# Batch 3's x loads, casts and transposing DMA moved ahead in a hand-ordered attention and maxout kernel on Trainium2

## The chip, the cores and the metric

The kernel runs on one core of a Trainium2 chip. The core has a matrix engine (TensorE, PE in the profile, with its weight loads as PEld), a vector engine (VectorE, DVE), a scalar engine (ScalarE, ACT), a general engine (GpSimd, POOL) and a sync engine (SyncE, SP), which here issues nearly all DMAs. Every engine works through its own list of instructions in program order and waits on semaphores for what other engines and DMAs deliver. The metric is device time in microseconds (us) of one execution; less is better.

## What is computed

```python
# x (8, 8, 512, 64), state (8, 8, 32, 64), float32
scores = scale * x @ state.T            # per batch and head
a      = softmax(scores)
xread  = a @ state                      # 512 rows
a2     = softmax(scale * state @ x.T)
sread  = a2 @ x                         # 32 rows
attn   = concat([xread, sread], axis=2) # then heads side by side: (8*544, 512)
h1, h2 = attn @ w1, attn @ w2
out    = maximum(h1, h2) @ w_out        # (4352, 512) float32
```

## The kernel before, in words

One pass handles one of the 8 batches. For batch n the kernel loads x (two DMAs of 512 KB, four heads each, `load_x`, line 164), casts it to bf16 twice, forms the scores, their exponentials, the weights a and their transpose, and multiplies the state with the maxout weights once for all (`sw`), so that the two matrix layers of the batch work from 64 rows of state and the transposed a.

The two casts have two users. `cast_e(b, k)` (name `ce` in the table, line 103 in the profile, tile `xe`) casts two heads into the tile that the product for sread reads; there are four of them for a batch. `cast_b(b, g)` (name `cb`, line 103 too, tile `xb`) casts four heads into the tile that is transposed; there are two. `xt_dma(b)` (name `xtd`, line 239) is a DMA that reads all of `xb` and writes the transposed x into `xt`. The score product `sc_mm` (line 261) reads `xt`. So a batch's scores need both loads, both `cb` and `xtd`; its four `ce` are needed only later, by `sr_mm` (line 301).

Tile `xt` has two buffers, `xe` three, `xb` two. The big float buffers are shared: x of batch 3 lies in a buffer of its own until output 3 takes it, x of batch 4 takes over one that held half of w2, and x of batch 7 takes the one that held output 0. `store(b)` (line 470) is the 1 MB DMA of a batch's output.

Nothing reorders the program: the order in which the code calls the helpers is each engine's order. For the weights and batches 0 and 1, with the parts of batches 2 to 5 that run beside them, this order is the table ORDER (lines 23 to 45), read from left to right by the loop at line 647. A token is a name with its batch and part, a letter behind ">" chooses the engine (A is ACT, V is DVE, P is POOL), and a number behind "@" the PSUM bank. After the table, the loop at line 736 writes passes b = 2 to 6: first layer of batch b (`l1_mm`, line 377: 16 matmuls), then the scores of batch n = b + 1 (line 261), then products of the second layer (lines 428 and 434), the state product (line 354), sread (line 301). So the first thing that needs batch 3's transposed x is the score product in pass b = 2, right behind the 16 matmuls of line 377. `cb` of batch 4 and its `xtd` are written ahead of that pass (lines 734 to 739), behind the x loads of batch 5 (`ldx.5`), the last tokens of the table.

The names of buffers in the order listings: big_118 holds x of batch 3, big_110 x of batch 4, big_113 x of batch 5, big_109 output 0; xe_84, xb_90 and xt_88 are the tiles of batch 3, a_93 and at_101 those of batch 2; big_115 holds the differences of two halves of `sw` (`difference`, line 404).

Of the kernel before, what the change touches and what calls it, by code (L numbers as in the profile page):

```python
# [35 lines left out]
sw.1.0@0,5 swe.0.0.0>A swe.0.0.1>V sw.0.w@1,3 sw.1.w@7,6 cb.2.1>P swe.1.0.0>A swe.1.0.1>V xtd.2 wt.1>P p2.1@2 l1.0.6@4  # L36
swe.0.w.0>A re.0.6>V l1.0.3@0 l1.0.2@5 swe.0.w.1>A re.0.3>V swe.1.w.0>V mS.1>A l1.0.1@4 l1.0.0@1 p2.0@3 swe.1.w.1>V
mS.0>A Sd dif.0>P re.0.2>V re.0.1>A re.0.0>A p2o.0 l1.1.0@7 l1.1.1@6 l1.1.2@0 l1.1.3@5 re.1.0>V re.1.1>A re.1.2>A
rs.0.0>V rs.0.1>V re.1.3>A p2o.1 ldx.4.1 ldx.3.0 ldx.4.0 ldx.3.1 p1.0@1 k0.0>A p1.1@4 rs.0.2>V wt.2>V v00.0 p6.0
rs.0.3>V k0.1>A k1.0>A p5.0@7 wt.3>V v00.1 rs.1.0>V k2.0>A sc.2.0@6 exp.2.0>A sc.2.1@0 exp.2.1>A sw.2.0@5,3 red.2.0>V  # L40
mul.2.0>P red.2.1>V swe.2.0.0>A swe.2.0.1>A ce.2.0>A ce.2.1>A ce.2.2>A ce.2.3>A p7.0 o7.0 v11.0 rs.1.1>V mul.2.1>P
p3.0 o3.0 rs.1.2>V atd.2 sw.2.w@6,2 swe.2.w.0>A v01.0 swe.2.w.1>A p4.0 o4.0 rs.1.3>V ce.3.0>P ce.3.1>P cb.3.0>P
ce.3.2>P ce.3.3>P cb.3.1>P v10.0>A store.0 xtd.3 dif.1>P sr.2@0 p6.1 k1.1>A sw.2.1@5,3 sre.2>V swe.2.1.0>A swe.2.1.1>V
p5.1@7 k2.1>A p7.1 o7.1 v11.1 p3.1 o3.1 v01.1 srt.2@0 srte.2>A p4.1 o4.1 v10.1>A ldx.5.0 ldx.5.1
"""

# [860 lines left out]
```

## Time and profile before

| what | us |
|---|---|
| median of 3 runs | 144.87 |
| the runs | 144.87, 231.15, 144.86 |
| profiled execution, its own time | 144.49 |
| its span in the trace | 142.7 |

The span is what the trace covers, from the first to the last instruction; the profiled execution's own time is 1.79 us more. The page lists, for each engine, how long it was busy, and for each stretch that one asks for the busy time in it. A wait is named by the engine that waited and by what released it. The chain is followed back from the last instruction: at each step, what released it. Matmuls are pipelined and their ends are modelled, so the starts of two matmuls tell more of PE's pace than the end of one.

### The profile page before, as it was taken

To read this page: it belongs to the slowest core of one execution; us is meant where nothing else is said; L and a number is where in the kernel's file an instruction comes from. 1 tells how busy PE (TensorE), PEld (TensorE's weight loads), DVE (VectorE), ACT (ScalarE), POOL (GpSimd) and SP (SyncE) were. 2 spreads that over 40 slices of the span, in tenths; PEclk is the share of its full clock that TensorE was granted. 3 is DMA by queue.
4 is the path that set the end of the run, shared out by engine and by line. 5 is a ranking of instruction groups with operands and counts; after the bars stand their busy time and mean duration, and the time that the engine had idled before them with its cause. 6 is when DMAs were issued, how large, how long until landed. Compare 5 with 4: busy or idle time off the path is not lost.

```text
span 142.7 us, 3661 instructions
## 1 busy us (share of the span) xinstructions
PE 134.8 (94%) x1442; PEld 95.1 (67%) x1442; DVE 104.5 (73%) x193; ACT 88.2 (62%) x172; POOL 72.4 (51%) x99
## 2 busy tenths in 40 slices
PE   6897999999999998999999999999999999999980
PEld 2475735456887764786678577857876786788860
DVE  3489979778999947974898489569948986847420
ACT  4357969887599445674874769086737745753220
POOL 4147335099019992699079909963980544200000
PEclk9999999999999999999999999999999999999999
DMA  4999999945999889979936999659217041502073
GB/s 128 337 365 395 387 384 386 341 80 102 179 330 276 299 172 293 135 189 275 403 129 122 211 356 199 146 207 238 43 38 294 2 78 71 225 0 78 12 246 119
DMA packets 36453, 29.50 MB, mean 207 GB/s; under 512 B 22609, under 2 KB 32337, under 8 KB 35537
## 3 DMA queue, kind: packets, MB, share of 16 engines
q1 hardware_dynamic: 36160, 29.10, 72.1%
q8 instruction: 12, 0.20, 0.5%
q10 hardware_dynamic: 272, 0.13, 0.3%
q14 instruction: 9, 0.07, 0.1%
HBM read 15.20 MB, written 8.91 MB: 169 GB/s over the span
## 4 chain that ended last, share of the span: by engine, by line
PE 75%; DMA 8%; DVE 5%; POOL 5%; ACT 2%; issue 2%; SPq 0%; POOLq 0%; DVEq 0%
PE bank L428 28%; PE bank L377 16%; PE bank L434 8%; PE bank L608 5%; DMA xt<-xb 4%; DVE big L404 4%; PE bank L354 4%; DMA big<-in_x_dram 3%; PE bank L261 3%; PE bank L475 2%; PE bank L517 2%; POOL xe L103 2%; PE bank L323 1%; POOL xb L103 1%; PE bank L550 1%
## 5 line engine op out<-in xcount | busy, mean ns | idle before, releaser
L277 POOL TENSOR_TENSOR a<-e,er 128x512 bf16<-128x512 bf16 x14 | 17.2, 1235 | 28.3 <-ACT big L99 20.9
L372 DVE TENSOR_SCALAR r<-bank 128x512 bf16<-128x512 f32 x32 | 21.9, 690 | 13.0 <-PE bank L377 12.6
L99 ACT COPY big<-bank 128x512 f32<-128x512 f32 (+2 forms) x40 | 21.8, 551 | 13.2 <-PE bank L434 5.5
L377 PE MATMUL bank<-at,sw 128*128 128x512 bf16 x128 | 29.5, 379 | 0.2 <-DVE sw L101 0.2
L428 PEld LDWEIGHTS <-big 128*128 128x128 bf16 x256 | 23.8, 97 | 6.1 <-DVE big L404 1.7
L99 ACT CAST sw<-bank 128x512 bf16<-128x512 f32 x36 | 20.1, 609 | 6.0 <-PE bank L354 6.0
L428 PE MATMUL bank<-big,big 128*128 128x256 bf16 x192 | 23.1, 273 | 0.1
L404 DVE TENSOR_TENSOR big<-bank,big 128x512 f32<-128x512 f32 (+1 forms) x25 | 16.5, 663 | 8.2 <-PE bank L434 7.8
L377 PEld LDWEIGHTS <-sw 128*128 128x128 bf16 x128 | 12.2, 97 | 13.5 <-ACT sw L99 0.5
L370 ACT ACTIVATE r<-bank 128x512 bf16<-128x512 f32 x32 | 18.3, 596 | 4.1 <-PE bank L377 3.9
L428 PEld LDWEIGHTS <-r 128*128 128x128 bf16 x192 | 18.2, 98 | 2.7 <-issue 0.5
L103 POOL CAST xe<-big 128x512 bf16<-128x512 f32 x23 | 16.2, 736 | 6.4 <-DMA big<-in_x_dram 6.4
L428 PE MATMUL bank<-wo,r 128*128 128x256 bf16 x128 | 15.5, 273 | 0.0
L103 POOL CAST xb<-big 128x1024 bf16<-128x1024 f32 x12 | 12.2, 1035 | 4.7 <-DMA big<-in_x_dram 4.7
L434 PE MATMUL bank<-sw,at 128*128 128x256 bf16 x96 | 14.4, 273 | 0.0
L99 ACT COPY sread_t<-bank 128x128 bf16<-128x128 bf16 x8 | 3.2, 472 | 17.3 <-PE bank L338 14.0
L434 PEld LDWEIGHTS <-at 128*128 128x128 bf16 x128 | 12.5, 98 | 1.7
L404 DVE TENSOR_TENSOR big<-r 128x1024 bf16<-128x1024 bf16 x16 | 11.6, 723 | 0.6
L273 DVE TENSOR_REDUCE sums<-e 128x16 f32<-128x512 bf16 x16 | 10.8, 675 | 0.3 <-ACT e L269 0.2
L269 ACT ACTIVATE e<-bank 128x512 bf16<-128x512 f32 x16 | 8.9, 596 | 3.2 <-PE bank L261 2.8
L404 POOL TENSOR_TENSOR big<-sw 128x512 bf16<-128x512 bf16 x8 | 9.2, 1151 | 1.3 <-issue 1.3
L101 DVE CAST sw<-bank 128x512 bf16<-128x512 f32 x12 | 7.9, 682 | 1.1 <-PE bank L354 1.1
(100 smaller groups left out, 186.9 us busy)
## 6 DMA issues: line engine op xcount, KB each, us to landing
big<-in_x_dram SPq DMA_DIRECT2D x14, 512.0 KB, 6.7
out_dram<-big SPq DMA_DIRECT2D x7, 1024.0 KB, 4.5
big<-in_moe_w_dram SPq DMA_DIRECT2D x8, 512.0 KB, 11.3
big<-in_moe_w_out_dram SPq DMA_DIRECT2D x4, 512.0 KB, 10.9
big<-in_x_dram SPq DMA_DIRECT2D x1, 1024.0 KB, 6.8
out_dram<-big SPq DMA_DIRECT2D x4, 256.0 KB, 2.8
sf<-in_state_dram SPq DMA_DIRECT2D x1, 384.0 KB, 10.4
out_dram<-w2m SPq DMA_DIRECT2D x2, 128.0 KB, 2.5
```

Of the source, the lines that this page charges most:

```text
L99: nc.scalar.copy(o, i)
L101: nc.vector.tensor_copy(o, i)
L103: nc.gpsimd.tensor_copy(o, i)
L269: nc.scalar.activation(out=e_view(e_s[b % 2], hh).rearrange("p (g c) i n -> p g c (i n)", g=2), in_=p.rearrange("p (c g m) -> p g c m", c= ...
L273: nc.vector.tensor_reduce(es_all[:, b, hh], e_view(e_s[b % 2], hh), axis=AXX, op=ALU.add)
L277: (nc.gpsimd if eng == "P" else nc.vector).tensor_mul(e_view(a_s[b % 2], hh), e_view(e_s[b % 2], hh), er_s[b % 2][:, hh].unsqueeze(3).to_b ...
L370: nc.scalar.activation(out=o, in_=p, func=ACTF.Relu)
L372: nc.vector.tensor_scalar(o, p, scalar1=0.0, scalar2=None, op0=ALU.max)
L377: nc.tensor.matmul(p, sw_s[b % 3][:, g, f * 128:(f + 1) * 128], at_s[b % 3][:, g].rearrange("p c t -> p (c t)"), start=(g == 0), stop=(g = ...
L404: (nc.gpsimd if eng == "P" else nc.vector).tensor_tensor(o, i0, i1, op=op)
L428: nc.tensor.matmul(pv[c], lhs[:, f, 128 * c:128 * c + 128], rhs[:, f, :], start=first and f == 0 and (c == 0 or pv.split), stop=False, ski ...
L434: nc.tensor.matmul(pv[c], at_s[b % 3][:, g, 2 * i + c, :], rhs[:, g, :], start=False, stop=False, skip_group_check=True)
```

## The change

Three pieces of the table are written in another order; nothing is added, removed or given to another engine. The four x loads come as batch 3's two and then batch 4's two, in place of 4, 3, 4, 3. Of batch 3's six casts on POOL, the two `cb` come behind the first `ce`, in place of third and sixth. `xtd.3` comes right behind them, so ahead of `store.0`, in place of behind all six casts and `store.0`.

```diff
-rs.0.0>V rs.0.1>V re.1.3>A p2o.1 ldx.4.1 ldx.3.0 ldx.4.0 ldx.3.1 p1.0@1 k0.0>A p1.1@4 rs.0.2>V wt.2>V v00.0 p6.0
+rs.0.0>V rs.0.1>V re.1.3>A p2o.1 ldx.3.0 ldx.3.1 ldx.4.0 ldx.4.1 p1.0@1 k0.0>A p1.1@4 rs.0.2>V wt.2>V v00.0 p6.0
...
-ce.3.2>P ce.3.3>P cb.3.1>P v10.0>A store.0 xtd.3 dif.1>P sr.2@0 p6.1 k1.1>A sw.2.1@5,3 sre.2>V swe.2.1.0>A swe.2.1.1>V
+ce.3.1>P ce.3.2>P ce.3.3>P v10.0>A store.0 dif.1>P sr.2@0 p6.1 k1.1>A sw.2.1@5,3 sre.2>V swe.2.1.0>A swe.2.1.1>V
```

The lists of PE, DVE and ACT are the same before and after. On POOL the place is between the two multiplications for batch 2's weights and the difference of batch 1:

```order
 L277 TENSOR_TENSOR a_93<-e_91,er_95 128x8x64 x2
-L103 CAST xe_84<-big_118 128x2x4x64 x2
-L103 CAST xb_90<-big_118 128x4x4x64
-L103 CAST xe_84<-big_118 128x2x4x64 x2
-L103 CAST xb_90<-big_118 128x4x4x64
+L103 CAST xe_84<-big_118 128x2x4x64
+L103 CAST xb_90<-big_118 128x4x4x64 x2
+L103 CAST xe_84<-big_118 128x2x4x64 x3
 L404 TENSOR_TENSOR big_115<-sw_103 128x512
```

The two casts for the transposing DMA moved from third and sixth place to second and third; the difference still comes behind all six. On SP's queue the place is between the state's transposing DMA and the loads of batch 5:

```order
-L164 DMA big_110<-in_x_dram 128x4x256
-L164 DMA big_118<-in_x_dram 128x4x256
-L164 DMA big_110<-in_x_dram 128x4x256
-L164 DMA big_118<-in_x_dram 128x4x256
+L164 DMA big_118<-in_x_dram 128x4x256 x2
+L164 DMA big_110<-in_x_dram 128x4x256 x2
 L282 DMA_TRANSPOSE at_101<-a_93 128x8x128
+L239 DMA_TRANSPOSE xt_88<-xb_90 128x16x128
 L470 DMA out_dram<-big_109 128x2048
-L239 DMA_TRANSPOSE xt_88<-xb_90 128x16x128
 L164 DMA big_113<-in_x_dram 128x4x256 x2
```

Batch 3's loads moved to the head of the four, and its transposing DMA from behind the store of output 0 to ahead of it; the loads of batch 5 now follow the store directly.

More of the change, by code (lines that the diff above doesn't have):

```diff
@@ L38 @@
 mS.0>A Sd dif.0>P re.0.2>V re.0.1>A re.0.0>A p2o.0 l1.1.0@7 l1.1.1@6 l1.1.2@0 l1.1.3@5 re.1.0>V re.1.1>A re.1.2>A
-rs.0.0>V rs.0.1>V re.1.3>A p2o.1 ldx.4.1 ldx.3.0 ldx.4.0 ldx.3.1 p1.0@1 k0.0>A p1.1@4 rs.0.2>V wt.2>V v00.0 p6.0
+rs.0.0>V rs.0.1>V re.1.3>A p2o.1 ldx.3.0 ldx.3.1 ldx.4.0 ldx.4.1 p1.0@1 k0.0>A p1.1@4 rs.0.2>V wt.2>V v00.0 p6.0
 rs.0.3>V k0.1>A k1.0>A p5.0@7 wt.3>V v00.1 rs.1.0>V k2.0>A sc.2.0@6 exp.2.0>A sc.2.1@0 exp.2.1>A sw.2.0@5,3 red.2.0>V
 mul.2.0>P red.2.1>V swe.2.0.0>A swe.2.0.1>A ce.2.0>A ce.2.1>A ce.2.2>A ce.2.3>A p7.0 o7.0 v11.0 rs.1.1>V mul.2.1>P
-p3.0 o3.0 rs.1.2>V atd.2 sw.2.w@6,2 swe.2.w.0>A v01.0 swe.2.w.1>A p4.0 o4.0 rs.1.3>V ce.3.0>P ce.3.1>P cb.3.0>P
-ce.3.2>P ce.3.3>P cb.3.1>P v10.0>A store.0 xtd.3 dif.1>P sr.2@0 p6.1 k1.1>A sw.2.1@5,3 sre.2>V swe.2.1.0>A swe.2.1.1>V
+p3.0 o3.0 rs.1.2>V atd.2 sw.2.w@6,2 swe.2.w.0>A v01.0 swe.2.w.1>A p4.0 o4.0 rs.1.3>V ce.3.0>P cb.3.0>P cb.3.1>P xtd.3
+ce.3.1>P ce.3.2>P ce.3.3>P v10.0>A store.0 dif.1>P sr.2@0 p6.1 k1.1>A sw.2.1@5,3 sre.2>V swe.2.1.0>A swe.2.1.1>V
 p5.1@7 k2.1>A p7.1 o7.1 v11.1 p3.1 o3.1 v01.1 srt.2@0 srte.2>A p4.1 o4.1 v10.1>A ldx.5.0 ldx.5.1
```

## The prediction

> **What bounds the kernel now.** I read the page's head first, then busy time by stage, then the chain, then PE's waits.
>
> ```profile
> span 142.7 us, 3661 instructions
> PE 134.8 (94%) x1442; PEld 95.1 (67%) x1442; DVE 104.5 (73%) x193; ACT 88.2 (62%) x172; POOL 72.4 (51%) x99
> ```
>
> PE is busy 94% of the span. Where the rest lies shows in the stretches (columns: length, then busy time of PE, PEld, DVE, ACT, POOL, the granted clock, the share of the DMA engines, GB/s):
>
> ```profile
> 44.00:51.73 7.73, 7.73 (x104) 6.38 (x103) 6.57 (x11) 4.28 (x9) 7.48 (x10) 1.00 0.94 241
> 51.73:66.01 14.28, 13.61 (x166) 9.64 (x164) 10.37 (x20) 8.53 (x17) 10.15 (x12) 1.00 1.04 221
> 66.01:79.29 13.28, 13.28 (x166) 9.57 (x163) 10.18 (x19) 9.00 (x19) 8.85 (x10) 1.00 0.74 219
> ...
> 119.05:142.70 23.65, 19.45 (x164) 15.62 (x160) 11.11 (x23) 9.64 (x23) 2.59 (x4) 1.00 0.32 113
> ```
>
> The second row is pass b = 2: PE stands there for 0.67 us (14.28 against 13.61 busy). Ahead of it PE is never free, in the next pass neither, and the clock is full. The last row is the tail with its final stores, which the change doesn't touch. PE's longest waits outside the start-up, and the chain at that place (start, length, what):
>
> ```profile
> PE bank L261 <- DMA xt<-xb: 0.7, 1, 0.7
> ```
>
> ```profile
> 44.40 2.04 POOL xe L103 x2
> 46.44 0.98 POOL xb L103
> ...
> 48.99 0.98 POOL xb L103
> ...
> 50.00 6.08 DMA xt<-xb
> ...
> 56.13 0.64 PE bank L261 x16
> ```
>
> So pass b = 2 waits at line 261 for batch 3's transposed x. The chain behind it is POOL's six casts and then 6.08 us from the issue of the transposing DMA to its landing. From 56.13 to the end the chain runs through PE almost alone. What the wait costs is read from the starts on PE's timeline:
>
> ```profile
> 51.84 3.62 PE L377 MATMUL bank<-at,sw 128*128 128x512 bf16 x16
> 56.13 0.64 PE L261 MATMUL bank<-sbd,xt 128*128 128x64 bf16 x16 [0.67 <-DMA xt<-xb]
> ...
> 65.96 3.62 PE L377 MATMUL bank<-at,sw 128*128 128x512 bf16 x16
> 69.41 0.63 PE L261 MATMUL bank<-sbd,xt 128*128 128x64 bf16 x16
> ```
>
> In pass b = 3, where nothing is waited for, line 261 starts 69.41 - 65.96 = 3.45 us behind line 377. In pass b = 2 it is 56.13 - 51.84 = 4.29. The wait therefore costs 0.84 us, and without it line 261 would start at 51.84 + 3.45 = 55.29. This is a cap: the change makes no PE work shorter, and PE isn't waiting anywhere else near it. Everything hangs on whether the DMA lands by 55.29.
>
> **The loads.** Each of the four has its own issue, from 36.82 on, in the same list; only the addresses change places. Below stand the first alone, and the median of the first and the second:
>
> ```profile
> big<-in_x_dram SPq DMA_DIRECT2D x1, 512.0 KB, 4.9
> big<-in_x_dram SPq DMA_DIRECT2D x2, 512.0 KB, 5.2
> ```
>
> The first took 4.9, the median of the two is 5.2, so the second took 5.5. It was issued near 37.8 and was there near 43.3. After the change these two are batch 3's. POOL's timeline tells when they are used:
>
> ```profile
> 43.35 1.05 POOL L277 TENSOR_TENSOR a<-e,er 128x512 bf16<-128x512 bf16 x1
> 44.34 2.09 POOL L103 CAST xe<-big 128x512 bf16<-128x512 f32 x2
> 46.38 1.04 POOL L103 CAST xb<-big 128x1024 bf16<-128x1024 f32 x1
> 47.67 1.32 POOL L103 CAST xe<-big 128x512 bf16<-128x512 f32 x2 [0.25 <-DMA big<-in_x_dram]
> 48.94 1.03 POOL L103 CAST xb<-big 128x1024 bf16<-128x1024 f32 x1
> 49.94 1.15 POOL L404 TENSOR_TENSOR big<-sw 128x512 bf16<-128x512 bf16 x1
> 52.29 2.02 POOL L103 CAST xb<-big 128x1024 bf16<-128x1024 f32 x2
> ```
>
> Before, the fourth load was batch 3's second half, and POOL stood 0.25 us for it until 47.67. That wait goes. The fourth load will be batch 4's and land at the same 47.67; its first user is the cast at 52.29, or a little earlier, so 4 us of cover hide it. The loads cost nothing and only allow the next step.
>
> **The casts.** The multiplication ahead of them ends at 44.4 and is not moved. After it come one `ce` and the two `cb`: half of 2.09 is 1.02 from start to start, then 1.03 and 1.04. So the second `cb` ends at 44.34 + 1.02 + 1.03 + 1.04 = 47.43, against 49.97 before: 2.54 us earlier. The three `ce` behind it take some 0.6 each and end near 49.2, so the difference at 49.94 starts no later than before. Their own reader, the sread product of batch 3, comes in pass b = 2 behind the scores, so after 56, and has 6 us of cover.
>
> One thing is unsure: how long a `cb` takes at 45.4.
>
> ```profile
> L103 POOL CAST xe<-big x23: 604/609/1075, 6.4 to 103.6; 128x512 bf16<-128x512 f32 x23
> L103 POOL CAST xb<-big x12: 1029/1035/1044, 28.5 to 93.0; 128x1024 bf16<-128x1024 f32 x12
> ```
>
> The two `ce` at 44.34 took 1.07 each, where the median is 0.609; something stretched them by 1.76. All twelve `cb` took 1.03 to 1.04, the one at 46.38 included. The lower bound is 1.03, the upper 1.04 x 1.76 = 1.83. I take 1.03, since it is the tile's own row and has no exception in 12. With both at 1.83 they would end at 44.34 + 1.02 + 1.83 + 1.83 = 49.02, still 0.95 earlier than before.
>
> The Trainium skill (GPSIMD Engine Reference, Key points) says that GpSimd shares its SBUF interfaces with VectorE and contends with instructions that have two SBUF inputs; DVE has such additions at this place. By that rule the stretched value is the right one for the first `cb` at least. The twelve rows of `cb` don't show it, the two `ce` fit it. By the rule the sum below would still come out at 0.84, with less to spare.
>
> **The transposing DMA on SP's queue.** SP's timeline (start, time to issue):
>
> ```profile
> 44.42 1.61 SPq L282 DMA_TRANSPOSE at<-a  x1
> 46.63 0.36 SPq L470 DMA_DIRECT2D out_dram<-big  x1
> 50.00 1.79 SPq L239 DMA_TRANSPOSE xt<-xb  x1
> 51.84 1.78 SPq L164 DMA_DIRECT2D big<-in_x_dram  x2
> 54.34 5.30 SPq L239 DMA_TRANSPOSE xt<-xb  x1
> 61.10 1.24 SPq L282 DMA_TRANSPOSE at<-a  x1
> ```
>
> SP is free from 46.03 and will now wait for the second `cb`: issue at 47.45 instead of 50.00. Behind it stand the store of output 0 and the loads of batch 5. The store goes from 46.63 to 47.45 + 1.79 = 49.25, 2.6 us later; its buffer is next wanted by x of batch 7, loaded in pass b = 3, so not ahead of 65.96: this costs nothing. The loads of batch 5 go from 51.84 to about 49.65 and gain. `xtd` of batch 4 waits for its own casts, as before.
>
> How long will it take to land? The same kind of DMA, issued at 50.00, 76.39, 54.34 and 81.03 (median from issue to landing of the one):
>
> ```profile
> xt<-xb SPq DMA_TRANSPOSE x1, 6.1
> xt<-xb SPq DMA_TRANSPOSE x1, 4.5
> xt<-xb SPq DMA_TRANSPOSE x1, 7.3
> xt<-xb SPq DMA_TRANSPOSE x1, 10.0
> ```
>
> The slow two were issued right behind 1 MB of loads and behind a store. The first two had little ahead of them. What is ahead at 47.45, with the store gone, shows in the stretch just before the store began to move (last columns: DMA share and GB/s):
>
> ```profile
> 46.50:47.10 0.60, 0.60 (x12) 0.23 (x11) 0.60 (x2) 0.32 (x1) 0.60 (x1) 1.00 0.06 21
> ```
>
> The DMA engines had run empty: 21 GB/s. So the new place is like that of 50.00, empty ahead and a large transfer right behind. I take 6.1; the bounds are 4.5 and 10.0. Landing at 47.45 + 6.1 = 53.55, 1.74 us before PE asks at 55.29. Even 7.3 gives 54.75. The wait goes whole.
>
> **What is late next.** With pass b = 2 shifted by 0.84, line 377 of pass b = 3 starts at 65.96 - 0.84 = 65.12 and needs batch 3's transposed weights, issued at 61.10 before, right behind POOL's multiplications. They shift with the scores, to 60.26. The same kind of DMA, issued at 44.42, took
>
> ```profile
> at<-a SPq DMA_TRANSPOSE x1, 4.1
> ```
>
> and 60.26 + 4.1 is 64.4, provided SP is free: it was at 54.34 + 5.30 = 59.64. This holds with 0.7 us to spare. `xt` of batch 4, by the row of 54.34, was there at 61.6; PE asks at 68.6.
>
> **Sum.** Loads 0, casts 0 by themselves, store 0, wait at line 261 -0.84. Span 142.7 - 0.84 = 141.86; the profiled execution's own time is 144.49 (1.79 more than its span), so 143.65. That execution stood 0.38 below the median of the runs; on the median it is 144.87 - 0.84 = 144.03. That is 0.6%, within the 2% that a measurement of this kernel can tell from no change.
>
> **Rivals.** First, slower: the transposing DMA takes 10.0 us in its new place, as at 81.03, because 2 MB (the store and batch 5's loads) now follow it at once and share the DMA engines. It lands at 57.45, PE starts 1.32 later than before, and the median is 146.2. It decides from 56.13 - 47.45 = 8.7 us on. Against it stands that the slow ones had their traffic ahead. Chance 6%.
>
> Second, stretched casts: both `cb` take 1.83, the issue is at 49.05, and with 6.1 the landing at 55.15 still just does; with 7.3 it is 56.35, 0.2 later than before. The wait shrinks only in part: some 144.1 to 145.1, say 144.5. The rule of the skill named above speaks for it. Chance 8%.
>
> Third, a wait that takes its place: SP is held up by batch 4's transposing DMA beyond 61.0 (81.03's took 6.45 to issue by SP's row below), so batch 3's transposed weights come late and PE stands at line 377 of pass b = 3. Up to all 0.84 is given back: 144.87, no change.
>
> ```profile
> 81.03 6.45 SPq L239 DMA_TRANSPOSE xt<-xb  x1
> ```
>
> From 54.34 this would free SP at 60.79, and 60.79 + 4.1 is 64.9, before 65.12; so chance 6%.
>
> **How the numbers follow.** Forecast 80%, rivals 6, 8 and 6%. The predicted time is 144.0. The range goes from 143.6 (the sum against the profiled execution's own time is 143.65, so the 0.38 by which it stands below the median is taken in) to 144.95, which takes in no change and most of the second rival; the slower rival and a remainder of the second are left out. None of the cases reaches 2%: faster needs 142.0, slower 147.8. Faster 1%, within 96%, slower 3% for a transposing DMA later than any row shows.
>
> **What would show it.** Right: POOL's two `cb` back to back ending near 47.4; SP's row of line 239 near 47.45 and the store near 49.25; no wait of PE at line 261 for the DMA; the stretch of pass b = 2 near 13.4 with PE busy throughout. Wrong: a cast above 1.1, a landing beyond 8 us, or a wait of PE at line 377 in pass b = 3.

## The result, and the profile after

| | us |
|---|---|
| before, median of 10 runs | 144.95 |
| changed, median of 10 runs | 143.99 |
| ratio, with its 95% interval | 0.9949 [0.9929, 0.9969] |
| profiled execution of the changed kernel, own time and span | 143.72 and 141.9 |

The changed kernel is 0.5% faster. That is within 2%, and clear of no change by its interval. The single run of 231 us of before is left out of the ratio.

The timeline of PE in the changed kernel, at the rows that were shown of before (a few matmul records are missing, so x15 stands for 16):

```profile
52.05 3.62 PE L377 MATMUL bank<-at,sw 128*128 128x512 bf16 x15
55.51 0.63 PE L261 MATMUL bank<-sbd,xt 128*128 128x64 bf16 x16
...
65.33 3.62 PE L377 MATMUL bank<-at,sw 128*128 128x512 bf16 x15
68.79 0.63 PE L261 MATMUL bank<-sbd,xt 128*128 128x64 bf16 x16
```

Line 261 now starts 55.51 - 52.05 = 3.46 us behind line 377, as it does in the next pass; before it was 4.29. The wait of PE for the transposing DMA is gone, 0.83 us. Pass b = 2 itself starts 0.21 later than in the trace before (52.05 against 51.84): its start-up happened to be longer. Line 377 of the last pass starts 0.62 earlier, which is 0.83 less 0.21, so nothing was lost on the way. The tail brings the span to 0.8 less. In PE's waits only the start-up is left:

```profile
PE bank L550 <- ACT wb L99: 1.4, 1, 1.4
PE bank L577 <- DVE ones L580: 1.3, 1, 1.3
PE bank L246 <- ACT xe L99: 1.2, 1, 1.2
```

POOL's timeline and SP's in the changed kernel:

```profile
44.55 1.07 POOL L103 CAST xe<-big 128x512 bf16<-128x512 f32 x1
45.57 2.94 POOL L103 CAST xb<-big 128x1024 bf16<-128x1024 f32 x2
48.46 1.72 POOL L103 CAST xe<-big 128x512 bf16<-128x512 f32 x3
50.15 1.15 POOL L404 TENSOR_TENSOR big<-sw 128x512 bf16<-128x512 bf16 x1
```

```profile
48.54 1.92 SPq L239 DMA_TRANSPOSE xt<-xb  x1
50.56 0.94 SPq L470 DMA_DIRECT2D out_dram<-big  x1
51.55 1.60 SPq L164 DMA_DIRECT2D big<-in_x_dram  x2
54.55 6.18 SPq L239 DMA_TRANSPOSE xt<-xb  x1
```

The two casts of `xb` took 1.50 and 1.49 us, not 1.03, so the DMA was issued at 48.54 and not at 47.45 (0.21 of the 1.09 is the later start of the first cast, the rest the length of the two). But it landed after 4.3 us, not 6.1:

```profile
xt<-xb SPq DMA_TRANSPOSE x1, 4.3
```

The two errors pull opposite ways, and the DMA is there at 52.87, 2.6 us ahead of PE (55.51). Why 4.3 here and 6.1 before? The trace has 16 completion events for each DMA, one for each DMA engine that carried a part of it. Those of batch 3's transposing DMA, in us:

```
          issued   first of 16   fifteenth   sixteenth
before     50.00         54.40       54.54       56.08
changed    48.54         52.71       52.85       52.87
```

In the kernel before, 15 engines were through 4.5 us after the issue. PE waited for the sixteenth. The Trainium skill (DMA: Bandwidth & Descriptors, Why a DMA increments its semaphore by 16 and not by 1) says that each engine adds one when its own part is done and that only all 16 mean landed; the trace agrees: PE's line 261 started at 56.13, 0.05 behind the last.

What held the one engine? In the trace before, the packets of the tenth of a microsecond from 54.0 (columns: queue, kind, packets, MB, share of 16 engines):

```profile
q8 instruction: 1, 0.02, 58.2%
q1 hardware_dynamic: 10, 0.01, 35.4%
```

A single packet of 16 KB, of the kind that the profile calls instruction, started on one DMA engine at 54.04 and took 0.93 us. There are 12 of these in the run (page, part 3: 12, 0.20 MB), one about every 120 matmuls of PE's program. In the changed kernel this load starts at 53.79, after the DMA is through. This gave a theory beside the one of the prediction: **the wait was made by an instruction load, and the change gains by landing ahead of it**. The rival is that order alone (casts, store, neighbours in the queue) sets the landing. That the loads are of PE's program is an inference from their number; runs 5 to 10 put it to the test.

### The profile page after: what moved, and what is told of

It is laid out like the page before. It is cut to its first block, busy times and chain, and to the rows that moved or that the text cites. A ratio compares the mean times of both kernels' runs of the same rounds, so it can differ in the third digit from the quotient of the medians.

```text
span 141.9 us, 3651 instructions
## 1 busy us (share of the span) xinstructions
PE 132.1 (93%) x1432; PEld 93.6 (66%) x1442; DVE 103.9 (73%) x193; ACT 88.4 (62%) x172; POOL 72.6 (51%) x99
## 4 chain that ended last, share of the span: by engine, by line
PE 85%; DMA 6%; DVE 2%; SPq 2%; ACT 1%; issue 1%; DVEq 0%
PE bank L428 36%; PE bank L377 18%; PE bank L434 10%; DMA big<-in_moe_w_dram 6%; PE bank L354 5%; PE bank L608 5%; PE bank L475 2%; PE bank L517 2%; PE bank L261 2%; PE bank L301 2%; SPq L164 1%; PE bank L515 1%; DVE w2m L101 1%; DVE r L372 1%; PE bank L550 1%
## 5 line engine op out<-in xcount | busy, mean ns | idle before, releaser
L103 POOL CAST xe<-big 128x512 bf16<-128x512 f32 x23 | 15.6, 709 | 6.2 <-DMA big<-in_x_dram 6.2
L103 POOL CAST xb<-big 128x1024 bf16<-128x1024 f32 x12 | 13.1, 1111 | 4.7 <-DMA big<-in_x_dram 4.7
```

Of the source, the lines that this page charges most:

```text
L103: nc.gpsimd.tensor_copy(o, i)
```

## The experiments

The first four kernels undo parts of the change. Only the edited tokens of the table are shown.

**1. Only the loads moved.**

```diff
-p2o.1 ldx.4.1 ldx.3.0 ldx.4.0 ldx.3.1
+p2o.1 ldx.3.0 ldx.3.1 ldx.4.0 ldx.4.1
```

> Only batch 3's loads ahead of batch 4's. Theory (the landing of the transposing DMA follows its issue): POOL's wait of 0.25 us before the third cast of xe goes, the second cast of xb ends some 0.2 earlier, the DMA is issued near 49.8 instead of 50.0, still behind the store, and takes 6.1; PE still waits at line 261, about 0.6 of the 0.84 us remain, the median falls by 0.2. Rival (the store ahead holds the DMA until it has landed at 50.9): no gain at all, PE waits as before.

Ratio 1.0021 [0.9992, 1.0050]: no gain. POOL's wait of 0.25 us for the load is not in this trace, but it is not in those of runs 2, 4, 5, 7, 9 and 10 either, which have the old order of loads. Nor did its absence bring the DMA forward: the cast that had waited began at once and took longer beside a VectorE addition, and from the start of the first `ce` to the issue it was 5.67 us, as in the kernel before (5.66). The DMA's last engine was again 1.6 us behind the others, and PE waited 0.6.

**2. Only the transposing DMA ahead of the store.**

```diff
-v10.0>A store.0 xtd.3
+xtd.3 v10.0>A store.0
```

> Only the transposing DMA ahead of the store; loads and casts as before. Issue at 50.0 as before, since it waits for the last cast. Theory of the prediction (the order against the store is worth nothing, 6.1 us in either place): landing at 56.1, PE waits as before, no gain. Rival (the store ahead and the loads of batch 5 close behind are what made it 6.1; with the store behind it takes 4.3 as in the changed kernel): landing at 54.3, PE's wait at line 261 gone, the whole 0.84 us gained by this move alone.

Ratio 0.9996 [0.9967, 1.0025]: no gain. The DMA took 6.0 with the store behind it, so the rival falls as it was put: the store ahead was not what made it late. The theory's 6.1 was close, but not because order is worth nothing: 15 engines were through after 4.4, and the rest is the sixteenth engine.

**3. Loads and casts moved, the DMA left behind the store.**

```diff
-p2o.1 ldx.4.1 ldx.3.0 ldx.4.0 ldx.3.1
+p2o.1 ldx.3.0 ldx.3.1 ldx.4.0 ldx.4.1
...
-ce.3.0>P ce.3.1>P cb.3.0>P ce.3.2>P ce.3.3>P cb.3.1>P
+ce.3.0>P cb.3.0>P cb.3.1>P ce.3.1>P ce.3.2>P ce.3.3>P
```

> Loads and casts moved, the transposing DMA left behind the store. Issue near 48.5 as in the changed kernel, the store 2 us ahead of it. Theory of the prediction (issue plus 6.1): landing at 54.6, ahead of 55.3, the whole 0.84 gained. Rival (the DMA moves only when the store is through, near 51.0): landing between 55.4 and 56.1 as before, 0 to 0.7 gained, PE waits at line 261 for it.

Ratio 0.9984 [0.9950, 1.0018], which by time alone is no answer. In the profile the DMA took 7.1: 5.5 on 15 engines, because the store's 1 MB moved first, and 1.55 more on the sixteenth. It landed at 55.71, and line 261 started 3.60 behind line 377. So 0.15 us of the wait were left, and there was no room beyond that. Neither of the two expectations had both parts.

**4. Casts and DMA moved, loads in the old order.**

```diff
-ce.3.0>P ce.3.1>P cb.3.0>P ce.3.2>P ce.3.3>P cb.3.1>P v10.0>A store.0 xtd.3
+ce.3.0>P cb.3.0>P cb.3.1>P xtd.3 ce.3.1>P ce.3.2>P ce.3.3>P v10.0>A store.0
```

> Casts and transposing DMA moved, loads in the old order (batch 4's first half first, batch 3's second half last). The second cast of xb waits for its load at 47.7 and ends at 48.7 to 49.2, the DMA is issued at 48.8 to 49.2 and lands at 53.1 (4.3) to 55.3 (6.1). Both theories: the whole 0.84 is gained, the order of the loads is worth at most some tenths of landing and nothing of the time. Rival (the loads' order is what the gain needs): PE waits at line 261 and the time is within 0.3 of before.

Ratio 0.9944 [0.9917, 0.9971], the whole gain. The order of the loads is worth nothing that shows here: POOL did not wait for the late load, its two casts took 2.94 together as in the changed kernel, and the DMA was issued at 48.78.

The next six kernels are to move the instruction load and leave the order alone; the start-up changes with it. The start of the program has 8 dummy matmuls of 512 columns, while PE waits for the first loads. If some become more and smaller ones, all later work stands further on in PE's instruction stream, and each load comes earlier against the work.

**5. Kernel before, 60 matmuls more at the start.**

```diff
-fill.100@0 fill.101@1 fill.102@0 fill.103@1 fill.104@0 fill.105@1 fill.106@0 fill.107@1
+idle.8.0.64 idle.9.1.64 idle.8.0.64 idle.9.1.64 idle.8.0.64 idle.9.1.64 idle.8.0.64 idle.9.1.64
...
-nc.tensor.matmul(p[:, 0:z.shape[1]], z[:, 0:128], z, start=True, stop=True)
+nc.tensor.matmul(p[:, 0:z.shape[1]], wz[:, 0:128], z, start=True, stop=True)
```

> The kernel before, its order untouched; only the eight dummy matmuls of 512 columns at the very start, where PE waits for the first loads, become 68 of 64 columns, so that every later point of PE's program lies 60 matmuls further on in its instruction stream. New theory (in the trace before, 15 of the 16 DMA engines finished the transposing DMA at 54.5 and the sixteenth at 56.1, after a 16 KB instruction load on one engine at 54.0; such a load comes about every 120 matmuls, so it now comes 60 matmuls earlier, near 48): the DMA lands near 54.5, PE's wait at line 261 goes, 0.84 us faster with no order changed. Rival (the traffic beside the DMA, or its place behind the store, makes it late): landing at 56.1, PE waits as before, time as before.

The load came at 48.27. All 16 engines finished by 55.26, 4.3 us after the issue at 50.98, with the store ahead as before. PE's timeline in this run:

```profile
52.82 3.62 PE L377 MATMUL bank<-at,sw 128*128 128x512 bf16 x15
56.27 0.63 PE L261 MATMUL bank<-sbd,xt 128*128 128x64 bf16 x16
```

The distance is 3.45: the wait is gone with no load, cast, DMA or store reordered. The time didn't follow, 1.0055 [1.0019, 1.0090]. In this trace pass b = 2 began 0.98 later (52.82 against 51.84), which is 0.14 more than the wait had cost, and the stretch behind the last pass's line 377 was 0.4 longer. Most of the other executions took longer still than this one, which stays unexplained. So the distance bears the theory out, and the time doesn't.

**6. Changed kernel, 31 more**, with the same edit of the helper's line, as in runs 8 to 10.

```diff
-fill.100@0 fill.101@1 fill.102@0 fill.103@1 fill.104@0 fill.105@1 fill.106@0 fill.107@1
+idle.5.0.64 idle.5.1.64 idle.5.0.64 idle.5.1.64 idle.5.0.64 idle.5.1.64 idle.5.0.64 idle.4.1.64
```

> The changed kernel with the same edit at the start, but 39 small matmuls for the eight, 31 more in all, so that by the new theory the instruction load falls into the transposing DMA's flight, near 50 to 51. New theory: one of 16 engines finishes about 1.5 us behind the rest, the DMA takes about 5.9 instead of 4.3 and lands near 54.4, still ahead of PE's 55.5: no wait at line 261, time as the changed kernel. Rival: landing 4.3 after the issue as in the changed kernel.

The load came at 49.18, just behind the issue at 49.00, earlier than aimed at. All engines finished together after 4.4. The expected 5.9 failed: a load at the very start of the flight does not set one engine back. Ratio 0.9954 [0.9925, 0.9983], as the changed kernel.

**7. Kernel before, fewer rows at the start.** `fill.200` and up are float32, 256 columns.

```diff
-fill.100@0 fill.101@1 fill.102@0 fill.103@1 fill.104@0 fill.105@1 fill.106@0 fill.107@1
+fill.200@0 fill.201@1
...
-fill.108@4
...
-fill.109@3 fill.110@4
+fill.209@3
```

> The kernel before, its order of loads, casts, DMAs and stores untouched; of the 11 dummy matmuls at the start (512 columns, bf16) the first eight become two of 256 columns in float32, one is left out and the last two become one, so that every later point of PE's program lies 19 rows of its list nearer the start. New theory (one 16 KB instruction load on one DMA engine makes the transposing DMA's last sixteenth 1.55 us late): the load now comes 1 to 2 us later against PE's line 377, after the DMA is through; the DMA takes 4.5 from its issue, PE starts line 261 at 3.45 us behind line 377, the wait is gone; if the start-up is not longer, 0.84 us faster than before with no order changed. Rival (the order of casts and store is what counts): the DMA takes 6 us, PE starts line 261 4.2 us behind line 377, time as before.

The edit didn't do what it was for: the load still came 2.17 us behind line 377 (54.84), as in the kernel before. With the load in the same place the old picture is there whole: 15 engines by 55.34, the sixteenth at 56.88, line 261 4.26 behind line 377. Ratio 1.0050 [1.0027, 1.0074]; in the trace the start-up lost 0.8, and PE stood 0.26 at line 377 of pass b = 5 for another DMA (`at`).

**8. Changed kernel, 7 more.** 

```diff
-fill.107@1
+idle.8.1.64
```

> The changed kernel with the last of the eight dummy matmuls of 512 columns at the start split into 8 of 64, 7 more in all, so that the instruction load comes about 1.5 us earlier, into the last part of the transposing DMA's flight. New theory: 15 of 16 DMA engines are through near 4.3 us after the issue, the sixteenth 1.5 later, near 54.4; PE asks at 55.5 and does not wait; time as the changed kernel. Rival (the load harms only what has loads or a store ahead or close behind): landing 4.3 after the issue.

The load came at 53.65, 15 engines were through by 54.10 and the last at 54.31: 0.21 behind, not 1.5. This speaks against a fixed price for a load near the end. Ratio 0.9939 [0.9916, 0.9963], and no wait of PE, as expected.

**9. Kernel before, 7 more**, the same edit.

> The kernel before with its order untouched and the last of the eight dummy matmuls of 512 columns at the start split into 8 of 64, 7 more in all, the same edit as in the run after_hit. The instruction load is then called for about 1.5 us earlier, while the transposing DMA is in mid-flight. Theory A (the load costs the DMA 1.55 us only where it falls into its last half microsecond): the load starts by 53, all 16 engines finish within 0.3 us, the DMA takes 4.5, PE starts line 261 at 3.45 to 3.6 us behind line 377, and if the start-up is as long as before, some 0.8 us are gained with no order changed. Theory B (a load called for at any time in the flight waits for the end of that engine's share and then delays its completion): one engine finishes 1.5 us behind as before, line 261 4.2 us behind line 377, time as before. Rival (order): time and wait as before, all engines late together.

The load came at 51.80, in mid-flight. All 16 engines finished by 55.70, 0.15 us apart, 5.1 after the issue; line 261 was 3.46 behind line 377. Theory A, then, with a price of some 0.6 us on all engines for a load in mid-flight. Ratio 0.9979 [0.9953, 1.0006]; pass b = 2 began 0.56 later than in the trace before.

**10. Kernel before, 21 more.**

```diff
-fill.105@1 fill.106@0 fill.107@1
+idle.8.1.64 idle.8.0.64 idle.8.1.64
```

> The same with three of the eight split, 21 more matmuls: the load is called for 4 to 4.5 us earlier than in the kernel before, at 49.5 to 50, when the store of output 0 moves and the transposing DMA has not begun. Theories A and B: the transposing DMA takes 4.3 to 4.6 on all 16 engines, PE starts line 261 at 3.45 us behind line 377, the wait is gone with no order changed, and the time falls by 0.8 less what the start-up loses to the smaller matmuls. Rival (order): the DMA takes 6, line 261 4.2 behind line 377, time as before.

The load came at 50.92, right behind the issue, and the DMA took 4.5 on all engines. SP's and PE's rows in this run:

```profile
50.68 3.12 SPq L239 DMA_TRANSPOSE xt<-xb  x1
```

```profile
52.52 3.62 PE L377 MATMUL bank<-at,sw 128*128 128x512 bf16 x15
55.97 0.63 PE L261 MATMUL bank<-sbd,xt 128*128 128x64 bf16 x16
```

The wait is gone again (3.45) in the old order, and the time falls, 0.9973 [0.9950, 0.9996], by half of what the change gains; in the trace the start-up is 0.7 longer than before.

**11. Changed kernel, the DMA behind 2 MB**, the first rival of the prediction with the traffic ahead instead of behind.

```diff
-cb.3.1>P xtd.3
+cb.3.1>P
...
-v10.0>A store.0
+v10.0>A store.0 ldx.5.0 ldx.5.1 xtd.3
...
-v10.1>A ldx.5.0 ldx.5.1
+v10.1>A
```

> The changed kernel with the transposing DMA behind both the store of output 0 and the loads of batch 5, 2 MB ahead of it in SP's queue. Issue near 49. Theory (what is ahead in the queue must move first): it moves from about 53 and lands at 56.4, or 1.5 later if an instruction load hits it; PE waits 1 to 2.5 us at line 261; time 0.2 to 1.5 us above the kernel before, 1 to 2.3 above the changed one. Rival (place in the queue doesn't matter, only the instruction load does): landing by 55.7, time as the changed kernel or up to 0.3 above.

The DMA took 9.6 and landed at 58.71, on all engines together. PE's row:

```profile
58.76 0.45 PE L261 MATMUL bank<-sbd,xt 128*128 128x64 bf16 x5 [3.07 <-DMA xt<-xb]
```

Ratio 1.0222 [1.0157, 1.0286] over 4 runs. So the place in the queue does matter, by what stands ahead. The time rose by 3.6 us (148.66 against 145.02), more than expected: by the starts, line 261 came 6.69 - 3.45 = 3.2 later than without a wait, and not at most 2.5. Another part came behind the wait, where nothing was waited for: from line 261 to line 377 of pass b = 3 PE took 70.11 - 58.76 = 11.35 us, against 65.96 - 56.13 = 9.83 before. The granted clock in this stretch and in the next (third number from the end, columns as in the prediction) gives the size of it:

```profile
58.70:70.10 11.40, 11.34 (x146) 8.97 (x147) 7.26 (x15) 5.66 (x12) 8.26 (x9) 0.86 0.60 154
70.10:83.38 13.28, 13.23 (x164) 9.59 (x163) 10.18 (x19) 9.01 (x19) 8.15 (x10) 1.00 0.66 200
```

It was 0.86 behind the wait of 3.07 us, and 9.83 / 0.86 is 11.4; in the next pass it was 1.00. In the kernel before, behind its wait of 0.67, it stayed at 1.00. That the long wait brought the clock down fits this, but no run tests it.

**12. Both casts of `xb` ahead of all of `xe`**, in one execution.

```diff
-ce.3.0>P cb.3.0>P cb.3.1>P xtd.3 ce.3.1>P
+cb.3.0>P cb.3.1>P xtd.3 ce.3.0>P ce.3.1>P
```

> The changed kernel with both casts of xb ahead of all four of xe. Theory (each POOL cast that meets one of VectorE's additions with two bf16 inputs in SBUF waits 0.46 us for it, whatever the cast): 1.50 us for each of the two, end and issue near 47.5, landing near 51.9. Rival (the stretch of 0.46 belongs to the casts of xe at the head, or to the tile): 1.04 each, issue near 46.7. Both: no time gained over the changed kernel, since PE doesn't wait there.

144.24 us in one execution, so nothing more is gained. POOL's rows of this run, and VectorE's beside them:

```profile
45.04 2.95 POOL L103 CAST xb<-big 128x1024 bf16<-128x1024 f32 x2
47.93 2.74 POOL L103 CAST xe<-big 128x512 bf16<-128x512 f32 x4
```

```profile
44.19 1.45 DVE L404 TENSOR_TENSOR big<-big,r 128x1024 bf16<-128x1024 bf16 x1
45.57 1.52 DVE L404 TENSOR_TENSOR big<-r 128x1024 bf16<-128x1024 bf16 x1
47.01 0.68 DVE L404 TENSOR_TENSOR big<-bank,big 128x512 f32<-128x512 f32 x1
47.61 0.92 DVE L404 TENSOR_TENSOR big<-r,big 128x1024 bf16<-128x1024 bf16 x1
```

Each `cb` took 1.50. Of the four `ce` the first, at 47.93, met the addition at 47.61 and took 1.07; the other three met none and took 0.61 each. The stretch belongs to the moment, not to the tile: the theory held.

The completions of batch 3's transposing DMA in all kernels, with the start of the instruction load nearest to it and the distance from the start of line 377 to that of line 261 (3.45 without a wait):

```
                 issued   load    fifteenth  sixteenth   line 261 behind 377
before            50.00   54.04      54.54      56.08      4.29
1 loads_only      50.64   54.57      55.04      56.63      4.21
2 dma_only        50.35   54.31      54.78      56.33      4.20
7 before_fewer    50.83   54.84      55.34      56.88      4.26
3 loads_casts     48.66   53.67      54.16      55.71      3.60
8 after_hit       49.66   53.65      54.10      54.31      3.45
9 before_7more    50.56   51.80      55.69      55.70      3.46
10 before_21more  50.68   50.92      55.16      55.17      3.45
6 after_shift     49.00   49.18      53.43      53.44      3.46
5 before_shift    50.98   48.27      55.26      55.26      3.45
changed           48.54   53.79      52.85      52.87      3.46
4 casts_dma       48.78   54.00      53.06      53.07      3.46
12 cb_first       48.01   56.38      52.29      52.30      3.46
11 dma_last       49.14   55.58      58.71      58.71      6.69
```

In five rows the sixteenth engine is 1.54 to 1.59 us behind the fifteenth, and in each of the five a load started 0.47 to 0.50 ahead of the fifteenth. Where the load lay elsewhere, all engines finished together. One row, `after_hit`, has the load at 0.45 and a lag of 0.21 only. Why that one escaped stays open; the trace doesn't name the DMA engine of a packet.

The other transposing DMAs of these 14 traces say the same and set a limit to it. Of all 182, eight have a sixteenth engine that is 1.49 to 1.59 us late; no other lags by more than 0.35. Each of the eight has a load that started 0.47 to 0.59 ahead of its fifteenth engine. But a load there doesn't always do it: with one at 0.39 to 0.63, seven of eight DMAs of line 239 were late, and only one of nineteen of line 282. So every long lag comes with such a load, and what else it takes is not known. Nor is why the engine loses 1.55 us by a packet that takes 0.93.

## Why the prediction was right, and where it was not

**What bounds, and the cap: right.** PE waits at line 261 in pass b = 2 and nowhere near; the cap of 0.84 was met with 0.83. That 144.0 was met with 143.99 is luck in the last digits: the median of before moved from 144.87 to 144.95, and the ten runs of the changed kernel lie between 143.68 and 144.84.

**The loads: right that they cost nothing.** That they "only allow the next step" was too much: without them (run 4) the step works as well.

**The casts: mis-sized.** The prediction took 1.03 for each `cb`, "since it is the tile's own row and has no exception in 12". They took 1.50 and 1.49, so one of its own signs of being wrong, a cast above 1.1, came up. The `cb` at 46.38 of before had begun just ahead of a VectorE addition, and there it was the addition that took long:

```profile
46.49 1.48 DVE L404 TENSOR_TENSOR big<-r,big 128x1024 bf16<-128x1024 bf16 x1
```

The two stretched `ce` stood in the very place to which the first `cb` was moved, and were the nearer rows. The stretch was not a factor of 1.76 but 0.46 us for each instruction: 0.61 to 1.07 for `ce`, 1.04 to 1.50 for `cb`. The rule of the Trainium skill that was weighed there (GPSIMD Engine Reference, Key points) gave the better answer.

**The landing: mis-sized, and for a wrong reason.** "Empty ahead and a large transfer right behind. I take 6.1." Emptiness ahead was right and counts (4.3 with nothing, 5.5 with 1 MB, 9.6 with 2 MB ahead and an instruction load in mid-flight), but 1.55 of the 6.1 were an instruction load that met the end of the flight. With 48.54 + 6.1 = 54.64 PE would still not have waited, so the conclusion stood on either number. With the 7.3 that the prediction also allowed it would not have: 48.54 + 7.3 = 55.84, behind PE's 55.51.

**What is late next: the conclusion right, the step wrong.** PE did not wait at line 377 of pass b = 3. But batch 3's transposed weights did not shift with the scores to 60.26. They were issued at 61.01, 0.09 earlier than before: VectorE reached the sums of the exponentials (line 273) at 57.11, straight from the addition at 56.50, where before it had waited 0.22 for ScalarE until 57.20. So VectorE's own list, which moves with line 377 and not with line 261, set the time. The DMA took 3.1, not 4.1, and was there at 64.13, 1.2 us ahead of line 377 (65.33).

**Rivals.** The stretched casts came true as a mechanism, and with a landing of 4.3 cost nothing. The DMA of 10 us did not come; run 11 took 9.6 with the traffic ahead. The hold on SP came in part: batch 4's transposing DMA took 6.18 to issue, not 5.30, and SP was free at 60.73, not 59.64. It cost nothing, since the weights were ready only then, with 0.3 us to spare. What the prediction lacked is the cause of the wait itself: the gain is the removal of a wait that one 16 KB packet had made. Without it the DMA of the old order would have been there near 54.54, by its other fifteen engines, ahead of 55.29. Both ways around it work, since runs 5, 9 and 10 lose the wait with the old order. The reordering is the better one: it puts 2.6 us between landing and use, and no start-up time is paid.

No kernel tried beats the changed one by more than the intervals.

## What to carry to other kernels

A wait for a DMA is to be read from its sixteen completions before it is put down to order or traffic: one engine 1.5 us behind the rest points to something on that engine, such as an instruction load. A DMA that lands just ahead of its use then depends on where PE's instruction stream stands, so that an edit elsewhere can make or break it; some 2 us of margin, here by casting first what the DMA reads, covers the 1.6 us that a load cost at most. And an operation's duration is to be taken from the rows at the place to which it moves, not from its own rows elsewhere.

## What the runs showed of the hardware that was not expected

**Instruction loads ride on the same DMA engines.** Packets of 16 KB, 12 in each of the traces of before and changed, 0.9 to 1.3 us each. For batch 3's transposing DMA such a load near the end of the flight left one engine 1.55 us behind in five traces of six, though line 282's DMAs mostly escaped; in mid-flight it cost some 0.6 on all (one trace, run 9), at the start 0.2 at most. The Trainium skill (Runtime: NRT & Kernel Launch, Instruction fetch mechanics) says that instructions are fetched in 16 KiB blocks through a DMA queue and that the cost is mostly hidden; the size agrees, but here one block cost the kernel 0.84 us, though PE waited there for data and not for an instruction.

**Of a GpSimd cast and a VectorE addition, the one that begins second waits for the other.** VectorE's additions of two bf16 inputs in SBUF (128x1024) took 0.69 us alone, `ce` 0.61 and `cb` 1.04. Where they met (us; "left" is what the first had still to run when the second began):

```
trace      first                    left   second              took, more than alone
before     addition 44.87           0.60   ce  45.36           1.07, 0.46
before     addition 46.49           0.30   ce  47.67           0.77, 0.16
changed    addition 45.08           0.60   cb  45.57           1.50, 0.46
cb_first   addition 47.61           0.59   ce  47.93           1.07, 0.46
before     ce 61.02                 0.34   addition 61.29      0.88, 0.19
before     cb 46.38                 0.93   addition 46.49      1.48, 0.79
cb_first   cb 45.04                 0.97   addition 45.57      1.52, 0.83
```

In each of these rows the second took longer by what was left of the first, less 0.13 to 0.15. So the 0.46 of the casts is such a remainder and no constant. The first was not lengthened by the meeting: the `ce` at 61.02 took 0.61, the `cb` at 46.38 1.04. What looks like a slow tile is the neighbour.

**The start-up varies by nearly as much as the effect.** In the eight profiled kernels whose start was not edited, line 377 of pass b = 2 began between 51.84 and 52.59, and the kernel before has the earliest. With 0.84 us at stake, the distance between two starts in one pass told more than the time of the run.
